# Turning and regrouping y with the first half of tanh, two buffers for the logits' copies, and another order of a chunk's steps

## The chip, the core and the metric

The kernel runs on one core of one Trainium2 chip. Its metric is the device time of one execution in microseconds. The engines of the core are TensorE (PE in the rows, with PEld for its weight loads), VectorE (DVE), ScalarE (ACT), GpSimd (POOL) and SyncE (SP), which issues nearly all transfers here.

## The reference, cut to what matters

```python
# 1. a spectral layer: rfft over 3072 positions, a complex 256x256 mix, soft threshold, irfft
y = np.fft.irfft(shrink(mix(np.fft.rfft(x, axis=1))), axis=1)     # (8, 3072, 256)
x = y.reshape(8 * 3072, 256)                                      # 24576 tokens
# 2. a gated layer without its own activation of the product
h = x @ w_in                                                      # 256 -> 2048
x = (h - np.tanh(h)) @ w_out                                      # 2048 -> 256
# 3. soft mixture of experts, 32 slots
logits = x @ phi
d = softmax(logits, axis=0)          # over the tokens
slot_input = d.T @ x                 # 32 x 256, then 8 small experts
c = softmax(logits, axis=1)          # over the slots
out = c @ slot_out
```

## The kernel before, in words

The program has three stages. `spectral_phase` computes y and stores it in DRAM. `token_phase` goes over the 24,576 tokens in 48 chunks of 512. `expert_phase` runs the experts on the 32 slots and writes the output. Nearly all the text below is about `token_phase`.

The layer after tanh is linear, so the kernel never forms `h - tanh(h)` for all tokens. It needs, for each chunk, g = tanh(h) (eight tiles of 128 x 2 x 512, numbered 0 to 7), the logits from g and from y, and a running sum over the chunks of exp(logits)-weighted g and y. The steps of a chunk c are:

- `P` (L777): products of y and w_in by a Winograd scheme, 28 groups of 6 matmuls; ACT copies the sums out (L788), `A` adds parts on DVE (L795), `G` is tanh on ACT (L799).
- `L` (L915, L923): the logits, from g tiles and from `yr`, a plain copy of y that `loadr` (L806) brings from DRAM.
- `sum`, `sum2`, `max`, `exp`, `turnexp`: the logits are copied to `le`, reduced, exponentiated, and turned to `et`. `comb`, `cexp` and `cend` make the other softmax from the same copy and store it (`ctd`, L1029).
- `T` (L866) turns a g tile by 32x32 blocks on DVE into `gt`; `TD` (L858) does the same with `yr`. There are two `gt` tiles: `gt0` takes tiles 0 to 3, `gt1` takes tiles 4 to 7 and, before the change, y.
- `reg` (L882), once for each half, moves the turned half by 16 transfers from SBUF to SBUF into four `gq` tiles, so that tokens stand on partitions. There are five `gq` buffers; a chunk takes four of them.
- `DY` (L837) multiplies `et` with the y part of `gq`, 32 small matmuls; `D` (L1045) multiplies `et` with the g part, 32 matmuls of 512 columns. They stand next to each other on PE, DY first. `accy` and `acc` add them to the running sums on DVE.

The order of the steps is written by hand in the table `PLAN`: each entry names a step, the chunk it belongs to (0 is the current one, -1 the one before, 1 the next) and which part. Each engine and each queue works its entries off in that order. DY and D of a chunk run near the end of the next chunk's entries. All transfers of this stage go out on SP's queue, one after the other; a transfer that has to wait for an engine holds up those behind it.

Of the kernel before, what the change touches and what calls it, by code (L numbers as in the profile page):

```python
# [9 lines left out]
F32 = mybir.dt.float32  # L10
# [8 lines left out]
S, D = 3072, 256  # L19
# [7 lines left out]


PLAN = (
# [8 lines left out]
    ("reg", -1, 1), ("W", 0, 3), ("splitt", 1, 0), ("comb", -1), ("P", 0, 3, 7),  # L38
# [3 lines left out]
)  # L42
TOKENS_BESIDE = {-4: 1, -2: 1, 0: 1, 1: 2, 2: 3, 3: 4}

# [595 lines left out]
def token_phase(tc, nch, yd, wh, wl, wp, wy, ident, ew):  # L640
# [9 lines left out]
    with ExitStack() as ctx:  # L650
# [73 lines left out]
        gt = {}  # L724
        banks = count()

        def bank():
            k = next(banks) % (4 if ps2 is None else 6)
            return (ps if k < 4 else ps2).tile([128, 512], F32, tag=f"b{k}", name="ph")
# [96 lines left out]
        def dy_mm(c):  # L826


            beside = c < nch - 1
            o = dy[c] = lp[c + 1][:, 256:320] if beside else bank()[:, 0:64]  # L830
            if beside:
                y = [g[:, 2048:2304].rearrange("p (k f) -> p k f", k=4) for g in gq[c]]
            else:
                y = [yq[c][:, a] for a in range(4)]
            for k in range(4):
                for a in (3, 2, 1, 0):
                    nc.tensor.matmul(  # L837
                        o[32 * a:32 * a + 32], ex[c][:, k, :], y[a][:, k], start=k == 0 and not beside, stop=k == 3,
                        skip_group_check=True,
                    )  # L840
# [7 lines left out]

        def gt_tile(c, h):
            if (c, h) not in gt:  # L850
                gt[c, h] = gtp.tile([128, 4, 1024 + 256 * h], F32, tag=f"gt{h}", name="gt", bufs=1)
            return gt[c, h]

        def turn_yr(c):

            t = gt_tile(c, 1)[:, :, 1024:1280].rearrange("p q (k f i) -> p q k f i", k=4, f=2)
            for kk in range(2):
                nc.vector.transpose(  # L858
                    out=t[:, :, :, kk, :], in_=yr[c][:, kk].rearrange("p (q k i) -> p q k i", q=4, k=4)
                )  # L860

        def turn_g(c, p):
            g = gs[c, p]
            t = gt_tile(c, p // 4)[:, :, 0:1024].rearrange("p q (k f i) -> p q k f i", k=4, f=8)
            for u in range(2):
                nc.vector.transpose(  # L866
                    out=t[:, :, :, 2 * (p % 4) + u, :], in_=g[:, u, :].rearrange("p (q k i) -> p q k i", q=4, k=4)
                )

        gq = {}  # L870
# [3 lines left out]
        def regroup(c, h):  # L874

            t = gt.pop((c, h))
            if h == 0:
                gq[c] = [ew.gq_tile([128, 2304]) for _ in range(4)]
            for a in range(4):
                o = gq[c][a][:, 1024 * h:1024 + 1280 * h]  # L880
                for q in range(4):
                    nc.sync.dma_start(out=o[32 * q:32 * q + 32], in_=t[32 * a:32 * a + 32, q])  # L882

# [47 lines left out]
        le = {}  # L931

        def sum_l(c):

            o = lp.pop(c)[:, 0:256]
            if c < nch - 1:
                le[c] = sp.tile([128, 256], F32, tag="le", name="le", bufs=1)
            else:

                last = ew.gp.tile([128, 384], F32, tag="g0", name="last")  # L940
                le[c], ew.rep = last[:, 0:256], last[:, 256:384]
            u = lr[c] = le[c][0:64]
            nc.scalar.activation(u, o[0:64], AF.Copy)
            lo[c] = o
# [88 lines left out]
        def dg_mm(c):  # L1033

            o = dp[c] = ps2.tile([128, 512], F32, tag="d", name="pd")
            if c < nch - 1:
                parts = [(
                    slice(0, 512), [g[:, 0:2048].rearrange("p (h k f) -> p k h f", h=2, k=4) for g in gq.pop(c)],
                )]
            else:  # L1040
                parts = [(slice(256 * h, 256 * h + 256), [gl[h][:, :, a] for a in range(4)]) for h in range(2)]
            for f, g in parts:
                for k in range(4):
                    for a in (3, 2, 1, 0):
                        nc.tensor.matmul(  # L1045
                            o[32 * a:32 * a + 32, f], ex[c][:, k, :], g[a][:, k], start=k == 0, stop=k == 3
                        )
            del ex[c]
# [14 lines left out]
        gtp = ew.gtp  # L1063
# [5 lines left out]
        def do(name, k, *args):  # L1069
            if (name, k, *args) not in done:  # L1070
                done.add((name, k, *args))
                calls[name](k, *args)
# [44 lines left out]
        c = 0  # L1117
        for s in range(8):
            p = FIRST[s]
            if s == 3:  # L1120
                ew.open_mid()
            if s == 5:
                ew.open_late()
                acc, accy, ssum = ew.acc, ew.accy, ew.ssum
                sp = pool("ts", 2)
# [16 lines left out]
            if s == 5:  # L1142
                do("splitt", 1, 0)
                do("splitt", 1, 1)
                split_sw(0)
                do("L", c, 0)
                do("L", c, 2)
            if s == 6:
                sum_w(1, nc.vector, ((ew.txp, "x2"), (ew.txp, "x3")))
                split_sw(1)  # L1150
                do("loadr", c)
                do("reg", c, 0)
                sum_w(2, nc.vector, ((ew.txp, "x0"), (ew.txp, "x1")))
                sum_w(3, nc.gpsimd, ((ew.txp, "x2"), (ew.gqp, "gq4")))
# [3 lines left out]
        c = nch - 1  # L1158
# [364 lines left out]
```

## Time and profile before

| | |
|---|---|
| median of 3 runs | 2242.1 us (2238.6 to 2248.22) |
| the profiled execution | 2236.65 us, span 2234.8 us |
| PE busy | 2169.0 us, 97% of the span |
| DVE busy | 1790.7 us, 80% |
| ACT busy | 1409.0 us, 63% |
| granted clock of TensorE, mean | 0.994 |

The profiled execution is one of several, and its own time is beside its span. Busy shares are averages over the three stages. The busy time of PE counts a matmul from its start to its modelled end, so short pauses between overlapping matmuls do not show in it.

### The profile page before, as it was taken

How to read it: one execution, taken by the hardware profiler on the slowest of the kernel's cores; microseconds unless marked ns; L12 is line 12 of the kernel's file. 1: busy time of each engine (PE TensorE's matmuls, PEld its weight loads, DVE VectorE, ACT ScalarE, POOL GpSimd, SP SyncE). 2: the span in 40 equal slices, each digit the busy share in tenths (PEclk: the TensorE clock that was granted, in tenths of full speed). 3: DMA queues.
4: the chain of work that ended last, by engine and by line, in shares of the span. 5: the costliest groups of instructions: out<-in, count | busy, mean ns of one | idle time of the engine just before them, and what ended most of it. 6: DMA issues, size and time to landing. Idle time of an engine off the chain costs nothing.

```text
span 2234.8 us, 50441 instructions
## 1 busy us (share of the span) xinstructions
PE 2169.0 (97%) x19456; PEld 1771.9 (79%) x19456; DVE 1790.7 (80%) x3651; ACT 1409.0 (63%) x2317; POOL 657.3 (29%) x666
## 2 busy tenths in 40 slices
PE   6999999999999999999999999999999999999998
PEld 3678888888888788888788888888888888888757
DVE  3999888988995888888788888888888888888634
ACT  2456666666555766766666667666666667666624
POOL 0343334444442322222222222222222222222111
PEclk8999999999999999999999999999999999999999
DMA  8778888888657788888788888888888888888999
GB/s 229 229 227 256 269 254 274 249 253 278 198 191 219 187 204 203 198 198 199 193 199 196 202 198 206 196 196 199 198 199 197 194 201 202 194 196 197 265 357 372
DMA packets 259631, 495.75 MB, mean 222 GB/s; under 512 B 36160, under 2 KB 159296, under 8 KB 259008
## 3 DMA queue, kind: packets, MB, share of 16 engines
q1 hardware_dynamic: 259280, 492.49, 81.4%
q8 instruction: 154, 2.52, 0.5%
q14 instruction: 85, 0.70, 0.1%
q10 hardware_dynamic: 112, 0.04, 0.0%
HBM read 164.45 MB, written 106.17 MB: 121 GB/s over the span
## 4 chain that ended last, share of the span: by engine, by line
PE 45%; SPq 8%; DMA 6%; DVE 6%; issue 1%; ACT 1%; POOL 0%; DVEq 0%; POOLq 0%; ACTq 0%
PE ph L777 25%; SPq L882 8%; PE pd L1045 7%; PE pl L915 7%; DMA gq<-gt 4%; DVE gt L866 3%; PE p_out L1344 3%; DVE g L795 2%; DMA ewt<-in_moe_w 2%; PE pl L837 2%; PE pl L923 1%; ACT g L788 1%; DMA gq<-wo 0%; DVE et L991 0%; DMA gq<-in_moe_w 0%
## 5 line engine op out<-in xcount | busy, mean ns | idle before, releaser
L788 ACT ACTIVATE g<-ph 128x512 f32<-128x512 f32 x752 | 447.5, 595 | 411.2 <-PE ph L777 380.6
L795 DVE TENSOR_TENSOR g<-ph,g 128x512 f32<-128x512 f32 x564 | 370.7, 678 | 170.2 <-PE ph L777 119.8
L777 PE MATMUL ph<-th,s 128*128 128x256 f32 x2256 | 486.3, 289 | 1.8 <-ACT g L788 1.8
L866 DVE STREAM_TRANSPOSE gt<-g 128x512 f32<-128x512 f32 x752 | 476.6, 681 | 13.0 <-DMA gq<-gt 6.6
L799 ACT ACTIVATE g<-g 128x1024 f32<-128x1024 f32 x376 | 396.3, 1054 | 32.7 <-DVE g L795 31.2
L777 PEld LDWEIGHTS ph<-th,s 128*128 128x128 f32 x2256 | 377.1, 189 | 35.3 <-issue 19.3
L777 PE MATMUL ph<-tl,s 128*128 128x256 f32 x1128 | 318.3, 282 | 0.0
L777 PE MATMUL ph<-y,wh 128*128 128x256 f32 x1128 | 315.7, 280 | 0.1
L777 PE MATMUL ph<-yh,wh 128*128 128x256 f32 x1128 | 314.9, 279 | 0.5 <-DVE g L795 0.5
L777 PE MATMUL ph<-yh,wl 128*128 128x256 f32 x1128 | 315.4, 280 | 0.0
L690 POOL TENSOR_TENSOR tl<-tr,th 128x512 fp32r<-128x512 f32 x94 | 122.2, 1300 | 378.1 <-ACT th L689 378.1
L372 POOL TENSOR_TENSOR sw<-t,c 64x256 f32<-64x256 f32 x192 | 169.6, 883 | 171.9 <-DVE c L364 141.6
L777 PEld LDWEIGHTS ph<-yh,wh 128*128 128x128 f32 x1128 | 213.0, 189 | 0.8 <-DVE g L795 0.8
L777 PEld LDWEIGHTS ph<-tl,s 128*128 128x128 f32 x1128 | 213.3, 189 | 0.0
L777 PEld LDWEIGHTS ph<-y,wh 128*128 128x128 f32 x1128 | 212.2, 188 | 0.4 <-POOL y L675 0.3
L777 PEld LDWEIGHTS ph<-yh,wl 128*128 128x128 f32 x1128 | 211.9, 188 | 0.0
L684 POOL TENSOR_TENSOR tr<-y 128x256 f32<-128x256 f32 x92 | 68.2, 741 | 424.1 <-DMA y<-yd 424.1
L915 PE MATMUL pl<-g,wp 128*32 128x256 f32 x3072 | 185.9, 382 | 0.0
L1045 PE MATMUL pd<-gq,et 128*32 128x512 f32 x1504 | 175.1, 595 | 0.0
L675 POOL TENSOR_TENSOR y<-y,yh 128x1024 fp32r<-128x1024 f32 x46 | 111.3, 2419 | 214.0 <-PE ph L777 213.9
L407 PEld LDWEIGHTS pi<-i,v 96*128 96x128 f32 x1024 | 127.6, 191 | 25.8 <-issue 20.8
L281 PEld LDWEIGHTS pf<-f,a 128*128 128x128 f32 x768 | 102.8, 196 | 54.4 <-issue 41.1
(224 smaller groups left out, 4467.4 us busy)
## 6 DMA issues: line engine op xcount, KB each, us to landing
gq<-gt SPq DMA_DIRECT2D x752, 160.0 KB, 3.6
gq<-gt SPq DMA_DIRECT2D x752, 128.0 KB, 2.3
xt<-in_x SPq DMA_DIRECT2D x64, 384.0 KB, 5.7
vd<-vs SPq DMA_DIRECT2D x96, 256.0 KB, 3.3
v<-vd SPq DMA_DIRECT2D x64, 384.0 KB, 5.2
yd<-yt SPq DMA_DIRECT2D x48, 512.0 KB, 5.8
y<-yd SPq DMA_DIRECT2D x48, 512.0 KB, 3.7
yr<-yd SPq DMA_DIRECT2D x48, 512.0 KB, 4.9
```

Source lines behind the costliest of these rows:

```text
L372: eng.tensor_tensor(out=v[64 * ri:64 * ri + 64, gg], in0=t[q, e], in1=c[q, e], op=ALU.subtract)
L407: nc.tensor.matmul(p[:, a, :], t[:, 4 * u + a, :], i2[:, 96 * n2:96 * n2 + 128], start=True, stop=True)
L675: eng.tensor_tensor(out=t, in0=yl.pop(c).bitcast(F32), in1=hi.bitcast(F32), op=ALU.subtract)
L690: nc.gpsimd.tensor_tensor(out=lo, in0=t, in1=hi.bitcast(F32), op=ALU.subtract)
L777: nc.tensor.matmul(o[:, 256 * j:256 * j + 256], a[u][:, 128 * j:128 * j + 128], y[v], start=new and j == 0 and k == 0, stop=n in (2, 3, 4) ...
L788: nc.scalar.activation(e[n], o.rearrange("p (j n) -> p j n", j=2), AF.Copy)
L795: nc.vector.tensor_tensor(out=h, in0=o, in1=h, op=ALU.add)
L799: nc.scalar.activation(g, g, AF.Tanh)
L866: nc.vector.transpose(out=t[:, :, :, 2 * (p % 4) + u, :], in_=g[:, u, :].rearrange("p (q k i) -> p q k i", q=4, k=4))
L882: nc.sync.dma_start(out=o[32 * q:32 * q + 32], in_=t[32 * a:32 * a + 32, q])
L915: nc.tensor.matmul(lp[c][q:q + 32, 0:256], wp[:, 2 * p + f, :], half_of(c, gs[c, p + f // 2][:, f % 2], h), start=p == 0 and f < 2, stop=F ...
L1045: nc.tensor.matmul(o[32 * a:32 * a + 32, f], ex[c][:, k, :], g[a][:, k], start=k == 0, stop=k == 3)
```

## The change

The y part of a chunk is turned into `gt0` instead of `gt1`, and goes to the first 256 columns of `gq` with the first half of tanh, instead of the last 256 with the second half. So the 16 transfers of the first half have 1280 columns instead of 1024, and those of the second half 1024 instead of 1280. DY reads the first 256 columns and D the other 2048. `le`, the copy of the logits, has two buffers instead of one. The table `PLAN` is rewritten as a whole; `loadr` now stands near its start and `TD` in its middle, where both stood near its end. In the first chunk, outside the table, `loadr` is issued one step earlier and `TD` runs ahead of the first regrouping.

```diff
-    ("P", 0, 0, 6), ("G", -1, 6), ("L", -1, 2), ("L", -1, 4), ("L", -1, 6), ("cend", -2), ("T", -1, 4), ("T", -1, 7), ("TD", -1), ("loady", 1), ("W", 0, 0),
+    ("S", 0, 2), ("loady", 1), ("T", -1, 4), ("T", -1, 7), ("G", -1, 6), ("W", 0, 0), ("P", 0, 0, 6), ("L", -1, 2), ("L", -1, 4),
...
-                y = [g[:, 2048:2304].rearrange("p (k f) -> p k f", k=4) for g in gq[c]]
+                y = [g[:, 0:256].rearrange("p (k f) -> p k f", k=4) for g in gq[c]]
...
-                gt[c, h] = gtp.tile([128, 4, 1024 + 256 * h], F32, tag=f"gt{h}", name="gt", bufs=1)
+                gt[c, h] = gtp.tile([128, 4, 1280 - 256 * h], F32, tag=f"gt{h}", name="gt", bufs=1)
...
-            t = gt_tile(c, 1)[:, :, 1024:1280].rearrange("p q (k f i) -> p q k f i", k=4, f=2)
+            t = gt_tile(c, 0)[:, :, 0:256].rearrange("p q (k f i) -> p q k f i", k=4, f=2)
...
-            t = gt_tile(c, p // 4)[:, :, 0:1024].rearrange("p q (k f i) -> p q k f i", k=4, f=8)
+            t = gt_tile(c, p // 4)
+            if p < 4:
+                t = t[:, :, 256:1280]
+            t = t.rearrange("p q (k f i) -> p q k f i", k=4, f=8)
...
-                o = gq[c][a][:, 1024 * h:1024 + 1280 * h]
+                o = gq[c][a][:, 1280 * h:1280 + 1024 * h]
...
-                le[c] = sp.tile([128, 256], F32, tag="le", name="le", bufs=1)
+                le[c] = sp.tile([128, 256], F32, tag="le", name="le", bufs=2)
...
-                    slice(0, 512), [g[:, 0:2048].rearrange("p (h k f) -> p k h f", h=2, k=4) for g in gq.pop(c)],
+                    slice(0, 512), [g[:, 256:2304].rearrange("p (h k f) -> p k h f", h=2, k=4) for g in gq.pop(c)],
...
                 do("L", c, 2)
+                do("loadr", c)
...
-                do("loadr", c)
+                do("TD", c)
                 do("reg", c, 0)
```

On SP, in a chunk in the middle of the token stage, the queue before reads as follows: the first half's regrouping (1024 columns), the store of the other softmax, the load of the next y, the second half's regrouping (1280 columns), the load of `yr`.

```order
L882 DMA gq<-gt 32x1024 x16
L1029 DMA ctd<-le 128x128
L664 DMA y<-yd_64 128x1024
L882 DMA gq<-gt 32x1280 x16
L806 DMA yr<-yd_64 128x1024
```

After the change it reads:

```order
L883 DMA gq<-gt 32x1280 x16
L662 DMA y<-yd_64 128x1024
L804 DMA yr<-yd_64 128x1024
L1030 DMA ctd<-le 128x128
L883 DMA gq<-gt 32x1024 x16
```

So the load of `yr` has moved from behind the second half's regrouping to ahead of it, and the store of `ctd` from ahead of y to behind `yr`.

On PE, the end of a chunk before, with what the instructions wait for (DMAHW are the semaphores of transfers): the last logits, DY, D, and the next P.

```order
L915 MATMUL pl<-g,wp 32x256 x8
L837 MATMUL pl<-gq,et 32x64 [waits DMAHW5_49,DMAHW4_49,DMAHW6_49,DMAHW3_49,DVE_49]
L837 MATMUL pl<-gq,et 32x64 [waits DMAHW2_49,DMAHW7_49,DMAHW1_49,DMAHW0_49]
L837 MATMUL pl<-gq,et 32x64 x14
L1045 MATMUL pd<-gq,et 32x512 x16
L777 MATMUL ph<-th,wh 128x256 [waits Activation_49]
```

The same place after the change:

```order
L916 MATMUL pl<-g,wp 32x256 x8
L835 MATMUL pl<-gq,et 32x64 [waits DMAHW5_49,DMAHW4_49,DMAHW6_49,DMAHW3_49,DVE_49]
L835 MATMUL pl<-gq,et 32x64 [waits DMAHW2_49,DMAHW7_49,DMAHW1_49,DMAHW0_49]
L835 MATMUL pl<-gq,et 32x64 x14
L1046 MATMUL pd<-gq,et 32x512 [waits DMAHW6_49,DMAHW7_49,DMAHW1_49,DMAHW0_49]
L1046 MATMUL pd<-gq,et 32x512 [waits DMAHW4_49,DMAHW5_49,DMAHW3_49,DMAHW2_49]
L1046 MATMUL pd<-gq,et 32x512 x14
L775 MATMUL ph<-th,wh 128x256 [waits Activation_49]
```

D has waits for transfers of its own now; before, everything it reads from `gq` had been waited for by DY.

On DVE, the rows around the last turned tile of the second half before (a `gt` row of shape 128x4x4x32 writes the 1280-column tile, L1023 to L1028 are `cend`, L858 is `TD`):

```order
L858 STREAM_TRANSPOSE gt<-yr 128x4x4x32 x2
L795 TENSOR_TENSOR g<-ph,g 128x2x256
L1023 TENSOR_REDUCE cz<-lt 128x4
L1024 TENSOR_SCALAR cz<-cz 128x4
L1025 RECIPROCAL cz<-cz 128x4
L1026 TENSOR_TENSOR lt<-lt,cz 128x128
L1028 STREAM_TRANSPOSE le<-lt 128x128
L866 STREAM_TRANSPOSE gt<-g 128x4x4x32 x4
L795 TENSOR_TENSOR g<-ph,g 128x2x256
L866 STREAM_TRANSPOSE gt<-g 128x4x4x32 x2
```

After the change (the second half is now the tile of shape 128x16x32):

```order
L867 STREAM_TRANSPOSE gt<-g 128x16x32 x2
L793 TENSOR_TENSOR g<-ph,g 128x2x256
L867 STREAM_TRANSPOSE gt<-g 128x16x32 x6
L1024 TENSOR_REDUCE cz<-lt 128x4
L1025 TENSOR_SCALAR cz<-cz 128x4
L1026 RECIPROCAL cz<-cz 128x4
L1027 TENSOR_TENSOR lt<-lt,cz 128x128
L1029 STREAM_TRANSPOSE le<-lt 128x128
L1054 SCALAR_TENSOR_TENSOR acc<-acc,al,pd 128x512
```

The last six transposes of the second half now stand together, ahead of `cend`, and `TD` has left this place.

## Rows read from the trace of the kernel before

**Rows 1.** The page: span, and the busy time of PE and DVE.

```profile
span 2234.8 us, 50441 instructions
PE 2169.0 (97%) x19456; PEld 1771.9 (79%) x19456; DVE 1790.7 (80%) x3651; ACT 1409.0 (63%) x2317; POOL 657.3 (29%) x666
```

**Rows 2.** Busy times in a window, the whole stretch of full chunks; columns first.

```profile
core 0: us, PE busy (x) PEld busy (x) DVE busy (x) ACT busy (x) POOL busy (x), PEclk, DMA share, GB/s
742.00:2077.00 1335.00, 1318.92 (x13696) 1090.77 (x13688) 1094.85 (x2297) 907.13 (x1441) 355.57 (x316) 1.00 0.82 198
```

**Rows 3.** The chain that ended last (start, length, what): some D, one late transfer.

```profile
743.22 3.43 PE pd L1045 x32
...
1094.40 3.65 DMA gq<-gt
1099.06 3.43 PE pd L1045 x31
...
1158.22 3.43 PE pd L1045 x31
...
1168.57 17.15 PE ph L777 x138
...
1187.29 3.43 PE pd L1045 x31
...
1216.51 3.43 PE pd L1045 x31
...
2077.99 3.43 PE pd L1045 x31
```

**Rows 4.** Timeline of PE: DY in two chunks, and the last (brackets: idle before).

```profile
1098.18 0.82 PE L837 MATMUL pl<-gq,et 128*32 128x64 f32 x29 [0.86 <-DMA gq<-gt]
...
1186.56 0.67 PE L837 MATMUL pl<-gq,et 128*32 128x64 f32 x29
1187.02 0.59 PE L1045 MATMUL pd<-gq,et 128*32 128x512 f32 x1
...
2110.78 1.20 PE L837 MATMUL pl<-gq,et 128*32 128x64 f32 x29 [3.42 <-DMA gq<-gt]
```

**Rows 5.** Timeline of SP: one second half, then the queue of another chunk.

```profile
1082.69 12.48 SPq L882 DMA_DIRECT2D gq<-gt  x16
...
1161.69 7.52 SPq L882 DMA_DIRECT2D gq<-gt  x12
...
1169.94 0.38 SPq L664 DMA_DIRECT2D y<-yd  x1
1172.07 11.30 SPq L882 DMA_DIRECT2D gq<-gt  x16
1183.47 0.69 SPq L806 DMA_DIRECT2D yr<-yd  x1
```

**Rows 6.** Timeline of DVE in that chunk, up to the second half's last transpose.

```profile
1164.02 0.69 DVE L795 TENSOR_TENSOR g<-ph,g 128x512 f32<-128x512 f32 x1 [1.73 <-PE ph L777]
1165.38 0.29 DVE L1023 TENSOR_REDUCE cz<-lt 128x4 f32<-128x128 f32 x1 [0.67 <-ACT lt L1018]
...
1166.44 0.31 DVE L1028 STREAM_TRANSPOSE le<-lt 128x128 f32<-128x128 f32 x1
...
1170.75 1.29 DVE L866 STREAM_TRANSPOSE gt<-g 128x512 f32<-128x512 f32 x2
```

**Rows 7.** The page: transfers by line, KB each, median us from issue to landing.

```profile
gq<-gt SPq DMA_DIRECT2D x752, 160.0 KB, 3.6
gq<-gt SPq DMA_DIRECT2D x752, 128.0 KB, 2.3
```

**Rows 8.** Window with the second half's transfers at work (columns as in rows 2).

```profile
1178.00:1184.00 6.00, 6.00 (x50) 5.71 (x49) 5.67 (x13) 5.64 (x11) 1.75 (x1) 1.00 0.98 228
```

**Rows 9.** Groups of ACT in the full chunks: busy, mean ns of one.

```profile
L788 ACT ACTIVATE g<-ph 128x512 f32<-128x512 f32 x720 | 428.5, 595 | 394.6 <-PE ph L777 366.7
L799 ACT ACTIVATE g<-g 128x1024 f32<-128x1024 f32 x361 | 380.6, 1054 | 31.3 <-DVE g L795 29.9
```

More of the change, by code (lines that the diff above doesn't have):

```diff
@@ L29 @@
 PLAN = (
[8 rows of a table removed]
-    ("reg", -1, 1), ("W", 0, 3), ("splitt", 1, 0), ("comb", -1), ("P", 0, 3, 7),
[3 rows of a table removed]
[10 rows of a table added]
 )
```

19 rows, old and new, of the table PLAN are left out of this document.

## The prediction

> **What bounds the kernel now.** I read the page first: PE is busy for 97% of the span and DVE for 80% [rows 1]. The time that a reordering can win is therefore PE's pauses and little else. The windows view shows where to look: the stretch of full chunks in the token stage take 1335 of 2234.8 us, with PE's granted clock at 1.00 throughout and the transfers at a share of 0.82 [rows 2]. The pauses that PE's busy time shows there are 16 us, but matmuls overlap, so a short pause is partly hidden in it.
>
> The chain gives the better measure. From D of the first full chunk to D of the last before the tail it is 2077.99 - 743.22 = 1334.77 us for 45 chunks, 29.66 us each. Where the chain runs through PE alone, a chunk takes less: 1158.22 to 1187.29 is 29.07, and 1187.29 to 1216.51 is 29.22 [rows 3]. So about 0.46 us of a chunk (29.66 - 29.20) is a wait, 45 x 0.46 = 20.7 us in all, and at most 45 x 0.59 = 26.6.
>
> The timeline of PE shows the place. In one chunk DY starts at 1098.18 after an idle time that a transfer into gq ended; the chain has that transfer from 1094.40 for 3.65 us, so it landed at 1098.05, 0.13 before DY. In another chunk DY starts at 1186.56 with no idle time [rows 3, 4]. What lands last is the second half's regrouping: its 16 transfers began at 1082.69 and their issue took 12.48 us; from first issue to last landing that is 15.36 us [rows 5]. And what starts them is DVE: in the chunk of 1158 the y load was issued at 1169.94 to 1170.32, then SP stood for 1.75 us until 1172.07, when the last transposes (1170.75 and 1.29) had ended [rows 5, 6]. Behind the waiting transfer nothing else could go. So the loop is: last P of a chunk, its addition and tanh, cend and six transposes on DVE, 16 transfers, DY.
>
> **The change, part by part.** DY no longer waits for the second half. Its columns come with the first half, which is issued a chunk's length earlier. The wait moves to D, and D's first matmul comes 0.46 us after DY (1187.02 - 1186.56) [rows 4]. That alone is worth the average wait: with the landing where it is, a chunk that waits 0.46 or less waits no more, and the one that waits 0.86 keeps 0.40. PE's own work is the same matmuls, so a chunk without a wait stays at 29.07 to 29.22.
>
> When does the second half land now? I count from D at 1158.22, so the next D's first matmul is due at 29.07 - 0.27 = 28.8 (the chain's row starts 0.27 after it). DY without a wait is 0.46 earlier, at 28.34, or 28.47 in a chunk of 29.20; before, DY came 0.46 later than that on average and the last landing 0.13 ahead of it, so the landing was at 28.8 as well.
>
> Gone is SP's wait for DVE, 1.75 us. cend, from 1165.38 to 1166.75 [rows 6], now stands behind the six transposes and delays only ctd. By DVE's rows the addition at 1164.02 comes about one P later (17.15 us for 23 groups, 0.75 each [rows 3]) and ends near 1165.5; six transposes (3 x 1.29) and cend (1.4) follow, so ctd is ready at about 1170.8, +12.6. SP ends its 12 copies at 1169.21, or 0.9 to 1.8 later by the third point, and y and yr take 0.38 and 0.69 more, so it reaches ctd at +13 to +13.9: DVE is no longer what SP waits for.
>
> Added ahead of the second half is the load of yr. Its issue is 0.69 us; 512 KB (128 x 1024 of 4 bytes) at the 228 GB/s of the busiest window [rows 8] are 2.3 us of the transfer engines. Lower bound of its cost 0.69, upper 2.3.
>
> The 12 first-half copies that wait for D carry 160 KB instead of 128. Twelve of 128 KB took 7.52 us, 0.63 each; sixteen of 160 KB took 11.30 to 12.48, 0.71 to 0.78 each [rows 5]. That is 0.9 to 1.8 us more.
>
> The 16 second-half copies carry 128 KB: 16 x (0.08 to 0.15) = 1.3 to 2.4 us less, and the last lands 2.3 us after its issue instead of 3.6 [rows 7], another 1.3 less when the queue is not full.
>
> With the transfer engines as the limit: -1.75 + 2.3 + 1.7 - 2.3 = -0.05, landing at 28.75. With SP's issue as the limit: -1.75 + 0.69 + 0.9 - 1.3 - 1.3 = -2.8, landing at 26.0. The bad end is slow issue in the first half (+1.8) with none of the relief in the second and 2.3 for yr: +2.35, landing at 31.1. I take 28.4: the share of 0.98 in the busiest window says that it is nearer to the first. That is 0.4 before D, and single chunks scatter by 1 us (15.36 from first issue to landing in one, at most 1186.56 - 1172.07 = 14.49 in another), so I keep 0.1 us a chunk, 4.5 us, as a remaining wait at D.
>
> A rule of the Trainium skill stands against this reading. The row has 228 GB/s at a share of 0.98 with mostly SBUF-to-SBUF copies at work [rows 8]. The page "DMA: Bandwidth & Descriptors", section "Where 436 GB/s comes from", says that such copies are bound by the fabric alone, at 435 GB/s. By it 160 KB would take 0.38 us, the issue would be the limit, the copies would have landed in time before and the change would win nothing; the row says that they are bound at about half that, and I go by the row.
>
> le with two buffers lets sum of a chunk stand ahead of the store of the chunk before. It costs nothing on any engine: copies, reductions and exponentials are as many as before. Its cover is that et must be there for DY. exp now comes after yh and two copies on ACT, then tanh of tile 0, its two transposes, and et. From P 2 6, which yh stands behind, to DY, PE has ten groups, 7.5 us, and the logits of two tiles. The chain on ACT and DVE is three copies (3 x 0.6), two tanh and yh (3 x 1.05), exp with two small companions (about one tanh), two transposes (1.3) and et (two of some 0.3, as L1028) [rows 6, 9]: 7.9 us. It is just hidden by the logits; without that cover each 0.1 us is 4.5 us in all.
>
> TD, T and A in another order: the same number on each engine; DVE is at 82% of this stretch (1094.85 / 1335) [rows 2], so it has 5 us a chunk to wait in. TD stands behind the maximum, two transposes and five additions that follow cend, some 7 us after yr's issue. I put this at nothing; the row of before that is nearest, a chunk of 29.22 without a transfer in its chain against 29.07, says up to 0.15 us a chunk for pauses of another kind, and a gain of as much is the other end.
>
> Ends. In the last chunk DY waits 3.42 us for the second half, which queues behind loads of expert weights [rows 4]. yr goes ahead of it now (+2.3) and its own bytes shrink (-2.3): no gain. The first chunk regroups only after TD. I allow 1 us for both.
>
> Sum: -20.7 + 4.5 + 1 = -15 us against the profiled execution's 2236.65 (span 2234.8 and 1.85 around it): 2221.5. That execution is 5.4 under the median of 2242.1, so the median becomes **2226**.
>
> **Rivals.** Rival 1, most of the wait comes back elsewhere: D waits in half the chunks, or et is late. For it: a margin of 0.4 us at D and hardly one at et. Against: D's part needs several rows at their bad ends. A wait of 0.25 to 0.4 a chunk leaves 3 to 9 us of gain: about 2236.
>
> Rival 2, no change. Either the idle time before DY was not the copies' but another wait's that stays, or D waits as long as DY did, with the landing at 29.3. Against the first: the landing 0.13 before DY [rows 3, 4]. For the second: it is 0.9 from my 28.4. 2242, plus or minus 5. The skill's rule of 435 GB/s would give the first of these; the trace agrees with it in no row shown here.
>
> Rival 3, slower, by SP's queue. From the end of D to the next D there are now 12 copies, y, yr, ctd and 16 copies in one line, and three of these wait for other engines. The same as before results when the landing is at 29.3; the bad end of 31.1 is past it. At 29.7, D comes 1.03 late and a chunk takes 30.1 and the kernel 45 x 0.46 = 20 us more: 2262. The same page of the Trainium skill, section "Anatomy of one DMA — SWDGE (gpsimd) path", says that the engines that move data do not wait on semaphores, only the issuing queue does; the 1.75 us pause of SP agrees.
>
> **Numbers.** Forecast 0.58 (2212 to 2233), rival 1 0.17, rival 2 0.10, rival 3 0.15. The range 2211 to 2250 holds the first three and the beginning of the last. About 0.5%, 11 us, is what a measurement of this kernel can tell from no change. Faster by more: 0.56 of the forecast and 0.06 of rival 1, 0.62. Within: 0.02, 0.11 and 0.08, 0.21. Slower: 0.17.
>
> **What would show it.** Right: DY follows the logits with no idle time in nearly all chunks, D's from one to the next average 29.2 to 29.35, SP goes from ctd to the second half without a pause, starting near +13.5 to +14.5. Wrong: idle time before D of 0.5 us or more on average (rival 3), PE waiting for ACT or DVE inside P (L775) or DY for et (rival 1), or DY still waiting.

## The result, and the profile after

The changed kernel takes 2206.48 us (median of 4 runs, 2203.23 to 2209.54), before 2242.16: a ratio of 0.9838, with a 95% interval of 0.9812 to 0.9864. The forecast was 2226 (2211 to 2250): the sign was right, the gain of 35.7 us is more than twice the 16 forecast, and the time lies under the range. Its profiled execution took 2206.43 us, as much as its median; that of the kernel before lies 5.5 us under its own, so between the two traces below the gain is 30.2 us.

The page, for [rows 1]; then the stretch of full chunks, for [rows 2]:

```profile
span 2204.5 us, 50535 instructions
PE 2140.2 (97%) x19456; PEld 1787.9 (81%) x19456; DVE 1826.2 (83%) x3651; ACT 1398.1 (63%) x2317; POOL 652.4 (30%) x666
```

```profile
744.00:2042.00 1298.00, 1285.43 (x13684) 1103.14 (x13680) 1127.02 (x2295) 896.53 (x1441) 350.78 (x316) 1.00 0.84 204
```

The shares of PE read the same, and the idle time left in the stretch (1298.00 - 1285.43 = 12.6 us, against 16.1) explains 3.5 us of the 37 by which the stretch is shorter (1335 to 1298). The chain shows what a chunk takes now, for [rows 3]:

```profile
744.96 3.67 PE pd L1046 x32
...
1464.92 3.67 PE pd L1046 x32
...
1493.38 3.67 PE pd L1046 x32
...
2043.08 3.85 PE pd L1046 x32
```

From the first to the last it is 1298.12 us for 45 chunks, 28.85 each, against 29.66. A chunk without a wait takes 1493.38 - 1464.92 = 28.46. The least in [rows 3] was 29.07, and the forecast kept that. The timeline of PE, for [rows 4]: one chunk without a wait, and one with it (its D is cut off by the end of the window).

```profile
1290.71 0.63 PE L835 MATMUL pl<-gq,et 128*32 128x64 f32 x32
1291.17 3.84 PE L1046 MATMUL pd<-gq,et 128*32 128x512 f32 x32
...
1319.16 0.63 PE L835 MATMUL pl<-gq,et 128*32 128x64 f32 x32
1320.02 2.31 PE L1046 MATMUL pd<-gq,et 128*32 128x512 f32 x17 [0.23 <-DMA gq<-gt]
```

DY waits for nothing in any of 47 chunks. D does in 26 of 45: here it starts 0.86 after DY instead of 0.46.

Where did the 37 us of the stretch go? On PE, from each matmul's start to the next one's, summed by line and averaged over chunks 2 to 43 (worked out from the start times of both traces):

| PE, us a chunk | before | after | x 45 |
|---|---|---|---|
| P | 20.884 | 20.197 | -30.9 |
| L, with DY's wait behind it | 4.553 | 4.047 | -22.8 |
| DY, with D's wait behind it | 0.658 | 0.810 | +6.8 |
| D | 3.576 | 3.789 | +9.6 |

The last two lines are best read as one: before, three of DY's rows start after D's first and cut its time short, and behind DY's first matmul stands a second wait for transfers (a step between its rows there of 0.18 as a rule, over 0.1 in 41 of 45 chunks, 0.01 to 0.06 in the others). After the change D has waits for transfers too. DY and D together take 4.23 on average before, and 4.23 after where D does not wait; so the 16.4 us that they cost more are nearly all D's wait, 0.35 a chunk.

P, the "same matmuls", gave most. The page can't show it: a matmul of P lasts 0.28 us and the next starts 0.117 later, so a pause of 0.15 is covered by the matmul before. It stands in the start times. Before, P 0 2 1 ends and P 0 1 4 begins, in the timeline of PE and then that of ACT:

```profile
1174.85 0.28 PE L777 MATMUL ph<-yh,wl 128*128 128x256 f32 x1
1175.12 0.38 PE L777 MATMUL ph<-th,wh 128*128 128x256 f32 x1
1175.34 0.28 PE L777 MATMUL ph<-tl,wh 128*128 128x256 f32 x1
```

```profile
1174.46 0.60 ACT L788 ACTIVATE g<-ph 128x512 f32<-128x512 f32 x1 [0.58 <-PE ph L777]
```

P 0 1 4 adds into the bank of P 0 1 7, and ACT reads that bank until 1174.46 + 0.60 = 1175.06. So the first matmul comes 0.27 after the one before instead of 0.117, and the second 0.22 after the first: 0.26 lost. The same happened ahead of P 0 3 6 (0.26). Ahead of P 0 2 7 (0.18) two groups stood between already (P 0 2 5 and P 0 1 3), but ACT had a tanh to do first, so its copy of P 0 2 6, whose last matmul starts at 1177.26, began only at 1178.23. The timeline of ACT before:

```profile
1177.26 1.06 ACT L799 ACTIVATE g<-g 128x1024 f32<-128x1024 f32 x1
1178.23 0.58 ACT L788 ACTIVATE g<-ph 128x512 f32<-128x512 f32 x1
```

P 0 2 7 begins at 1178.86, when that copy has ended (1178.81). The three together are 0.69 a chunk, 31 us. In the new order that tanh (`G 0 3`) stands behind the copy, and two groups instead of one stand between P 0 1 7 and P 0 1 4 and between P 0 3 1 and P 0 3 6. The place ahead of P 0 1 4 has no pause in the timeline of PE after:

```profile
1309.56 0.28 PE L775 MATMUL ph<-yh,wl 128*128 128x256 f32 x1
1309.68 0.28 PE L775 MATMUL ph<-th,wh 128*128 128x256 f32 x1
1309.80 0.28 PE L775 MATMUL ph<-tl,wh 128*128 128x256 f32 x1
```

Below, "excess inside P" is this loss: for each P group the time from the matmul ahead of it to its own last one, less six steps of 0.1167, summed over a chunk. It is 1.69 before and 1.00 after; about 0.82 is the two groups that follow D or the logits in both.

The rest is the wait at D. The timeline of SP in a chunk after, for [rows 5] (the 18 copies in the last row are 16 of this half and 2 of the next), what SP waited for (us in total, times, longest), and the transfers by line, for [rows 7]:

```profile
1303.88 0.69 SPq L662 DMA_DIRECT2D y<-yd  x1
1304.67 1.12 SPq L804 DMA_DIRECT2D yr<-yd  x1
1305.89 0.37 SPq L1030 DMA_DIRECT2D ctd<-le  x1
1306.32 15.25 SPq L883 DMA_DIRECT2D gq<-gt  x18
```

```profile
SPq L883 <- DMA yr<-yd: 65.7, 43, 3.5
```

```profile
gq<-gt SPq DMA_DIRECT2D x752, 160.0 KB, 3.4
gq<-gt SPq DMA_DIRECT2D x752, 128.0 KB, 3.6
...
y<-yd SPq DMA_DIRECT2D x48, 512.0 KB, 5.0
yr<-yd SPq DMA_DIRECT2D x48, 512.0 KB, 6.5
```

The second half starts 14.56 us after the first matmul of the D before (mean of 45), without a wait for DVE. But a copy of it then stands until yr has landed: 65.7 us, 1.5 a chunk. Nothing in that copy depends on yr; in the trace SP's transfers carry eight completion semaphores in turn, and the seventh copy, the eighth transfer behind yr, is the one that takes yr's again (here it starts at 1311.89, yr landed at 1311.88). The half's last landing comes 28.50 after D's first matmul (standard deviation 0.69), and D is due at 28.46.

### The profile page after: what moved, and what is told of

Same layout as the page of the kernel before. It is cut to its first block, busy times and chain, and to the rows that moved or that the text cites. A ratio compares the mean times of both kernels' runs of the same rounds, so it can differ in the third digit from the quotient of the medians.

```text
span 2204.5 us, 50535 instructions
## 1 busy us (share of the span) xinstructions
PE 2140.2 (97%) x19456; PEld 1787.9 (81%) x19456; DVE 1826.2 (83%) x3651; ACT 1398.1 (63%) x2317; POOL 652.4 (30%) x666
## 4 chain that ended last, share of the span: by engine, by line
PE 71%; DMA 12%; SPq 9%; DVE 5%; issue 2%; ACT 1%; POOL 0%; POOLq 0%; DVEq 0%; ACTq 0%
PE ph L775 28%; SPq L883 8%; PE pd L1046 8%; PE pl L916 6%; PE pmix L320 5%; DMA yr<-yd 5%; PE pi L405 5%; PE pf L246 4%; PE pf L279 3%; PE pi L377 3%; PE p_out L1346 3%; PE pa L320 3%; DMA gq<-gt 2%; DMA ewt<-in_moe_w 2%; DVE sw L370 1%
## 5 line engine op out<-in xcount | busy, mean ns | idle before, releaser
L786 ACT ACTIVATE g<-ph 128x512 f32<-128x512 f32 x752 | 440.4, 592 | 342.0 <-PE ph L775 321.4
L867 DVE STREAM_TRANSPOSE gt<-g 128x512 f32<-128x512 f32 x752 | 482.4, 683 | 38.3 <-ACT g L797 30.7
L775 PE MATMUL ph<-th,s 128*128 128x256 f32 x2256 | 477.3, 285 | 5.5 <-ACT g L786 4.5
L797 ACT ACTIVATE g<-g 128x1024 f32<-128x1024 f32 x376 | 390.4, 1052 | 1.8 <-DVE g L793 0.3
L1046 PE MATMUL pd<-gq,et 128*32 128x512 f32 x1504 | 183.0, 599 | 15.7 <-DMA gq<-gt 14.9
L1046 PEld LDWEIGHTS pd<-gq,et 128*32 128x32 f32 x1504 | 89.5, 110 | 71.4 <-issue 18.7
```

Of the source, the lines that this page charges most:

```text
L775: nc.tensor.matmul(o[:, 256 * j:256 * j + 256], a[u][:, 128 * j:128 * j + 128], y[v], start=new and j == 0 and k == 0, stop=n in (2, 3, 4) ...
L786: nc.scalar.activation(e[n], o.rearrange("p (j n) -> p j n", j=2), AF.Copy)
L797: nc.scalar.activation(g, g, AF.Tanh)
L867: nc.vector.transpose(out=t[:, :, :, 2 * (p % 4) + u, :], in_=g[:, u, :].rearrange("p (q k i) -> p q k i", q=4, k=4))
L1046: nc.tensor.matmul(o[32 * a:32 * a + 32, f], ex[c][:, k, :], g[a][:, k], start=k == 0, stop=k == 3)
```

## The experiments

All ratios are to the kernel before, on the same chip. P is named with chunk, column pair and product, as in the table `PLAN`. "Landing" is that of the second half after the first matmul of the D before, mean of 45 chunks.

**The order alone, and y alone.** First the new order with y in its old place (slices, `gt1` and start as before):

```diff
-("W", 0, 2), ("TD", 0), ("A", 0, 1, 3),
+("W", 0, 2), ("A", 0, 1, 3),
...
-("T", 0, 5), ("P", 1, 0, 2),
+("T", 0, 5), ("TD", 0), ("P", 1, 0, 2),
```

> The changed kernel's order of steps, but y is turned into gt1 and regrouped with the second half as before (1024 columns first, 1280 second, DY on the last 256 columns); TD of the current chunk stands behind T 0 5, its only step moved. Theory A (the order of the P groups took away three short pauses a chunk): the pauses ahead of P 0 1 4, P 0 2 7 and P 0 3 6 stay away and a chunk without a wait takes about 28.46 us, but DY waits for the second half again, by 0.5 to 1.5 us a chunk, so the time is 2215 to 2250. Theory B (the shorter chunk comes from the moved y transfers, not from the order): the pauses are back, a chunk without a wait takes 29.07 or more, and the time is 2240 or more.

2274.65 us, ratio 1.0138 (1.0116 to 1.0161): 31 us slower than before. The excess inside P is 0.99, so the order does take the pauses away. But with 1280 columns in the second half and yr ahead of it the landing is at 29.57, and DY waits 1.7 us a chunk, more than the 0.5 to 1.5 expected, so the time is over theory A's 2250 as well. What PE waited for:

```profile
PE pl L835 <- DMA gq<-gt: 59.9, 38, 3.6
```

Then the old order with y in the first half:

```diff
-("L", -1, 6), ("cend", -2), ("T", -1, 4), ("T", -1, 7), ("TD", -1), ("loady", 1),
+("L", -1, 6), ("loadr", 0), ("cend", -2), ("T", -1, 4), ("T", -1, 7), ("loady", 1),
-("W", 0, 2), ("A", 0, 1, 3),
+("W", 0, 2), ("TD", 0), ("A", 0, 1, 3),
...
-("loadr", 0), ("reg", 0, 0), ("G", 0, 7), ("A", 0, 3, 2), ("TD", 0),
+("reg", 0, 0), ("G", 0, 7), ("A", 0, 3, 2),
```

> The order table of before, with y turned and regrouped with the first half; loadr stands behind L -1 6 and TD behind P 0 2 7, since y has to be there for the first half; le keeps one buffer. Theory A: the three pauses stay, a chunk without a wait takes 29.07 to 29.2 us, DY waits no more and D by 0.1 a chunk at most, so 45 x (29.66 - 29.2) = 20 us are won: 2215 to 2228. Theory B: a chunk without a wait takes 28.46 and the time is about that of the changed kernel, 2206.

2250.98 us, ratio 1.0033 (1.0019 to 1.0047): slower, against both theories. DY waits no more and D hardly (0.02 a chunk), as expected, but the excess inside P is 2.37. The new part is 0.56 ahead of P 0 2 3, which waits for an addition that TD now holds up on DVE:

```profile
PE ph L777 <- DVE g L795: 12.8, 45, 0.3
```

(only what exceeds the matmul before counts there, so it reads 0.3 a chunk). So TD was put behind `T 0 0`:

```diff
-("W", 0, 2), ("TD", 0), ("A", 0, 1, 3),
+("W", 0, 2), ("A", 0, 1, 3),
...
-("T", 0, 0), ("G", 0, 2),
+("T", 0, 0), ("TD", 0), ("G", 0, 2),
```

> As the run of y alone, but TD stands behind T 0 0, so that it no longer holds up the addition that P 0 2 3 waits for (0.56 us a chunk there). Theory A: that pause is gone, the three old ones stay, a chunk takes 29.0 to 29.2 us with hardly a wait, and 45 x 0.5 = 22 us are won against before: 2216 to 2226. If instead y in the first half is worth nothing without the new order, the time stays at 2240 or more.

2233.61 us, ratio 0.9963 (0.995 to 0.9977). The three pauses stay (excess 1.86), D waits 0.16 a chunk, the landing is at 28.94. The 0.56 is gone, so TD's place was its cause. y's move in the old order is worth 9 us, less than half of what I expected, and the order alone costs 31; together they win 36. The order makes D due earlier, and y's move takes DY out of the way of the landing.

**The pauses put back.** First one, then all three, by exchanges of neighbours in the changed kernel:

```diff
-("P", 0, 2, 1), ("P", 0, 2, 2), ("P", 0, 1, 4),
+("P", 0, 2, 1), ("P", 0, 1, 4), ("P", 0, 2, 2),
```

> The changed kernel with one pair exchanged: P 0 1 4 ahead of P 0 2 2, so that one group instead of two stands between P 0 1 7 and P 0 1 4, which add into the same bank. Theory A: a pause ahead of P 0 1 4 comes back, a chunk in which D does not wait grows from 28.46 by 0.2 to 0.26 us, D waits less by nearly as much, and the time grows by 2 to 11 us. Theory B: no pause, 28.46, the same time.

2215.78 us, ratio 0.9877 (0.985 to 0.9904), 9 more than the changed kernel. The pause is there (0.25), a chunk without a wait takes 28.72, and D's wait did not shrink (0.34 a chunk, against 0.35): the landing came later too, at 28.76. The intervals of the two ratios touch; the runs themselves do not (2213 and more, against 2210 and less).

```diff
-("P", 0, 1, 3), ("P", 0, 2, 7),
+("P", 0, 2, 7), ("P", 0, 1, 3),
...
-("P", 0, 3, 2), ("P", 0, 3, 5), ("G", 0, 0), ("P", 0, 3, 6),
+("P", 0, 3, 5), ("G", 0, 0), ("P", 0, 3, 6), ("P", 0, 3, 2),
```

(and the exchange above)

> The changed kernel with all three pairs exchanged: P 0 1 4 ahead of P 0 2 2, P 0 2 7 ahead of P 0 1 3, P 0 3 2 behind P 0 3 6, so that one group stands between two that add into the same bank. If the missed part of the gain is these pauses, the excess inside P grows from 1.00 to some 1.7 us a chunk, a chunk without a wait takes 29.1 to 29.25, D waits 0.1 to 0.25 on average since the second half lands 28.5 us after the D before, and the time is 2206 + 45 x (29.3 - 28.85) = 2226, between 2222 and 2236: what was forecast for the change. If not, the time stays under 2215.

2227.35 us, ratio 0.9918 (0.9895 to 0.9941). Excess 1.70, 29.16 a chunk without a wait, D's wait 0.16, landing at 28.60: every number as expected. With a chunk of the length that I assumed, the kernel takes what I forecast for the change. (The pause ahead of P 0 2 7 is made here by one group between instead of two, and is 0.25; the one of before came from the tanh.)

**The pauses taken out of the kernel before.** Three tries, each with more entries moved:

```diff
-("P", 0, 2, 1), ("sum", -1), ("P", 0, 1, 4),
+("P", 0, 2, 1), ("sum", -1), ("P", 0, 2, 2), ("P", 0, 1, 4),
...
-("G", 0, 3), ("rawt", 1), ("sum2", -1), ("P", 0, 2, 2), ("P", 0, 2, 6),
+("rawt", 1), ("sum2", -1), ("P", 0, 2, 6), ("G", 0, 3),
...
-("lowy", 1), ("P", 0, 3, 6), ("turnexp", -1), ("T", 0, 3), ("P", 0, 2, 3),
+("lowy", 1), ("P", 0, 2, 3), ("turnexp", -1), ("T", 0, 3), ("P", 0, 3, 6),
```

> The kernel before with the three pauses alone taken out of the order: P 0 2 2 ahead of P 0 1 4, G 0 3 behind P 0 2 6, P 0 3 6 and P 0 2 3 exchanged. Theory A: the P groups lose some 0.7 us a chunk, but the second half still lands 28.8 us after D as its start hangs on D and DVE, so DY waits 0.5 to 0.7 longer and the time hardly moves: 2232 to 2243. Rival (the pauses are worth their length whatever stands around them): 45 x 0.69 = 31 us less, 2211.

2243.29 us, ratio 1.0003 (0.9988 to 1.0019). The time is as theory A had it, but not for its reason: the excess is 1.78, with 0.51 ahead of P 0 2 3 (an addition on DVE) and 0.29 ahead of P 0 2 6. The second and third try leave P 0 3 6 and P 0 2 3 in their order, and have these instead:

```diff
-("A", 0, 0, 3), ("G", 0, 0),
+("A", 0, 0, 3),
...
-("P", 0, 3, 1), ("A", 0, 2, 7), ("P", 0, 3, 5),
+("P", 0, 3, 1), ("G", 0, 0), ("A", 0, 2, 7), ("P", 0, 3, 2), ("P", 0, 3, 5),
...
-("P", 0, 2, 4), ("A", 0, 2, 3), ("P", 0, 3, 2),
+("P", 0, 2, 4), ("A", 0, 2, 3),
```

> The kernel before with the pauses alone taken out, in another way than the first time (there they came back elsewhere): P 0 2 2 ahead of P 0 1 4, P 0 3 2 ahead of P 0 3 5, G 0 3 behind P 0 2 6 and G 0 0 behind P 0 3 1, so that no tanh stands on ACT between a group and the copy that the next group of its bank waits for. Theory A: the pauses inside P sum to under 0.2 us a chunk instead of 0.70, and DY's wait grows by nearly as much, since the second half lands some 28.8 us after D as before: 2232 to 2243. Rival: the pauses are worth 31 us by themselves, 2213.

2241.15 us, ratio 0.9986 (0.9973 to 0.9998). Excess 2.02: ACT is late with its copies at the chunk's end, 0.76 ahead of P 0 3 7. The third try also moves tanh of tile 2:

```diff
-("G", 0, 2), ("lowy", 1), ("P", 0, 3, 6),
+("lowy", 1), ("P", 0, 3, 6), ("G", 0, 2),
```

> As the second try to take out the pauses alone, with G 0 2 behind P 0 3 6, so that ACT is not behind with the copies of P 0 3 6 and P 0 3 7. If the excess inside P falls under 1.2 us a chunk (1.69 before), the run tells: theory A, the second half lands 28.8 us after D's first matmul as before, DY's wait grows from 0.49 to 0.8 us or more a chunk and the time is 2230 to 2242; rival, the pauses are worth their length, 2211 to 2220. If the excess stays over 1.5, the run tells nothing of them.

2243.59 us, ratio 1.001 (1.0 to 1.0021). The old pauses are gone and 1.03 stands ahead of and in P 1 0 2 (ACT, and POOL's part of the split): excess 2.03. None of the three tells what the pauses are worth in the kernel before; that stays open. In each of them the pauses come back at other places, behind DVE, ACT or POOL.

**What D waits for.** Queue or bytes? The load of yr from POOL, then both loads:

```diff
-nc.sync.dma_start(out=t, in_=yd[c // 6][c % 6])
+(nc.gpsimd if 1 < c < nch - 1 else nc.sync).dma_start(out=t, in_=yd[c // 6][c % 6])
```

> The changed kernel, with the load of yr (chunks 2 to 46) issued by POOL instead of SP; nothing else moves. Theory Q (SP's line is what makes the second half late: its seventh copy stands until yr has landed, 1.5 us a chunk, and yr's issue costs 0.4 to 1.1 more): the second half's issue takes some 10.3 us instead of 12, it lands before D in nearly all chunks, D's wait falls from 0.39 us a chunk on average to 0.1 or less, and the time is 2190 to 2197. Theory T (the transfer engines are full there, shares of 0.9 to 1.06, and whichever queue asks, the bytes take as long): the landing stays, D waits 0.3 to 0.45 a chunk, 2203 to 2210.

2224.28 us, ratio 0.993 (0.9901 to 0.9959): slower than the changed kernel, so theory Q falls; theory T's time (2203 to 2210) was missed too. SP no longer stands for yr, but longer for y, whose median landing went from 5.0 to 7.6 us:

```profile
SPq L883 <- DMA y<-yd: 92.2, 45, 3.7
```

```profile
y<-yd SPq DMA_DIRECT2D x48, 512.0 KB, 7.6
yr<-yd POOLq DMA_DIRECT2D x45, 512.0 KB, 5.7
```

The landing is at 28.88 and D waits 0.59 a chunk. The Trainium skill says the same ("DMA: Bandwidth & Descriptors", section "Issuing engines are not separate DMA queues"): transfers of all issuers share the same engines, and a second issuer saves only the issuing time. The trace agrees: with yr off SP's line the second half lands no earlier (28.88, against 28.50).

The same edit in `load_y` as well:

> The changed kernel with both loads, y and yr (chunks 2 to 46), issued by POOL. Theory Q: as with yr alone or 1 to 4 us better, since SP issues 32 copies and ctd alone and no copy stands behind a 512 KB load: 2186 to 2196. Theory T: 2203 to 2210. If POOL is late in its line (it splits weights and y's low parts), y or yr come late and P or the logits wait: over 2215.

2270.87 us, ratio 1.0112 (1.0088 to 1.0136): the third case. The 16 copies take longer to issue (13.4 us, against 12.0), though hardly one stands behind y or yr any more; they stand behind earlier copies and ctd (83.7 and 30.6 us in all). And yr comes so late (8.4 us from POOL's issue) that TD blocks DVE and P 0 1 3 loses 1.2 us a chunk:

```profile
PE ph L775 <- DVE g L793: 44.0, 32, 2.9
```

So fewer bytes: the load of yr cut, then replaced.

```diff
+            n = 64 if 1 < c < nch - 1 else 512
+            if n == 64:
+                nc.gpsimd.memset(t[:, :, 64:512], 0.0)
-            nc.sync.dma_start(out=t, in_=yd[c // 6][c % 6])
+            nc.sync.dma_start(out=t[:, :, 0:n], in_=yd[c // 6][c % 6][:, :, 0:n])
```

> The changed kernel with the load of yr cut to 64 of 512 columns (POOL sets the others to zero), in chunks 2 to 46, at the same place of SP's line: the logits' and the softmax's y part are left out for the rest. It keeps the place in the line and takes away 448 KB. Theory T: as without the load, D waits under 0.05 us a chunk, 2188 to 2195. Theory Q (the place in SP's line): the landing moves by under 0.7 us, 2200 to 2206.

2189.63 us, ratio 0.9766 (0.9751 to 0.978): theory T. (The kernel leaves out most of y's part of the logits, so it only measures.) D waits 0.04 a chunk, no copy stands for yr, the 16 copies issue in 10.9 us, and the landing is at 27.73, which is 0.77 earlier. That is less than the 2 us that 448 KB take at the 228 GB/s of [rows 8]: the copies then go one behind the other at SP's pace, 0.68 us each on average.

```diff
-            nc.sync.dma_start(out=t, in_=yd[c // 6][c % 6])
+            hi, lo = ys[c]
+            nc.gpsimd.tensor_tensor(out=t, in0=hi.bitcast(F32), in1=lo.bitcast(F32), op=ALU.add)
```

> The changed kernel without the load of yr: POOL makes it as the sum of yh and of the low part of y, which lie in SBUF in the chunk that needs it. So 512 KB a chunk go from SP's line and from the transfer engines. Theory T (the second half is late since the transfer engines have too many bytes ahead of it): at 228 GB/s the 512 KB are 2.3 us, the second half lands 2 us earlier, D waits under 0.05 us a chunk instead of 0.35, and the time is 2188 to 2194. Rival (its landing hangs on D's end, DVE and SP's pace of 0.64 us a copy, not on bytes): the landing moves by 0.5 us at most and the time is 2200 to 2206; if POOL is late with yr, the logits or TD wait: over 2210.

2230.75 us, ratio 0.9947 (0.9929 to 0.9964), over both theories' ranges. The landing is at 27.73 too and D waits 0.01. But P 0 0 3 now waits 0.9 us a chunk for an addition on DVE. The timelines of DVE and POOL show why:

```profile
1346.67 0.18 DVE L1027 RECIPROCAL cz<-cz 128x4 f32<-128x4 f32 x1
1346.88 2.52 DVE L1028 TENSOR_TENSOR lt<-lt,cz 128x128 f32<-128x128 f32 x1
1349.44 0.31 DVE L1030 STREAM_TRANSPOSE le<-lt 128x128 f32<-128x128 f32 x1
```

```profile
1346.86 2.39 POOL L805 TENSOR_TENSOR yr<-yh,y 128x1024 f32<-128x1024 f32 x1 [2.69 <-issue]
```

cend's multiplication takes 0.29 us elsewhere and here as long as POOL's addition beside it. So cend was moved ahead of the last two transposes:

```diff
-("T", -1, 7), ("G", -1, 6),
+("T", -1, 7), ("cend", -2), ("G", -1, 6),
...
-("T", -1, 6), ("cend", -2), ("acc", -2),
+("T", -1, 6), ("acc", -2),
```

> The changed kernel with yr made on POOL, and cend moved from behind T -1 6 to behind T -1 7, so that its multiplication on DVE (2.52 us beside POOL's addition, 0.29 before) is done when POOL makes yr. If that was the cause of the pause of 0.9 us ahead of P 0 0 3, the pause goes, a chunk takes 28.46 to 28.55 us, D waits under 0.05, and the time is 2187 to 2194. If POOL holds up DVE's transposes and additions too, P still waits for DVE by 0.3 us or more a chunk: 2203 to 2225.

2190.41 us, ratio 0.9769 (0.9755 to 0.9784), and a chunk of 28.47: 16 us less than the changed kernel and 52 less than the one before. In its DVE and POOL timelines the two no longer meet, and the page has PE at 98%:

```profile
1325.20 0.29 DVE L1028 TENSOR_TENSOR lt<-lt,cz 128x128 f32<-128x128 f32 x1
```

```profile
1326.36 2.41 POOL L805 TENSOR_TENSOR yr<-yh,y 128x1024 f32<-128x1024 f32 x1 [2.69 <-issue]
```

```profile
PE 2135.3 (98%) x19456; PEld 1784.8 (82%) x19456; DVE 1826.6 (84%) x3651; ACT 1398.1 (64%) x2317; POOL 768.4 (35%) x714
```

**The ends.** In the changed kernel PE idles for 4.54 us at the start of chunk 1, where ACT's `split_sw` 2 waits for DVE ahead of the copies of P. That step was put back:

```diff
-("S", 0, 2), ("loady", 1),
+("loady", 1),
...
-("G", 0, 1), ("P", 0, 0, 3),
+("G", 0, 1), ("S", 0, 2), ("P", 0, 0, 3),
```

> The changed kernel with split_sw 2, which runs in chunk 1 alone, put back behind G 0 1, where it stood before. If its wait for DVE's sums at the start of chunk 1 is what holds the copies of P back there (PE idle for 4.53 us), the first DY comes 3 to 6 us earlier and the time is 2200 to 2204; the rival (the sums are late anyway and PE waits for them a few groups later): the same time within 1.5 us.

2212.61 us, ratio 0.986 (0.9845 to 0.9874): no gain, and over both cases; the interval overlaps that of the changed kernel. The timeline of PE has the wait in pieces and later:

```profile
724.21 0.39 PE L775 MATMUL ph<-th,s 128*128 128x256 f32 x1 [2.58 <-ACT g L786]
...
737.52 0.58 PE L775 MATMUL ph<-th,s 128*128 128x256 f32 x1 [5.19 <-ACT g L786]
```

The last chunk's load of yr, and its first expert loads, behind the regrouping:

```diff
-if k < nch - 1 or name not in ("T", "TD", "reg"):
+if k < nch - 1 or name not in ("T", "TD", "reg", "loadr"):
-("W", 0, 0), ("P", 0, 0, 6),
+("P", 0, 0, 6),
...
-("W", 0, 1),
+("W", 0, 1), ("W", 0, 0),
```

> The changed kernel with the last chunk's load of yr and the first loads of expert weights and ctd behind the second half's regrouping of the chunk before, in chunk 47 alone. If that line on SP is what holds the last D beside a full chunk up (3.6 us), it waits under 0.5 us and the time is 1 to 4 us less, 2202 to 2205; the rival (the experts then wait for those loads at the end): no gain, 2205 to 2210.

2205.74 us, ratio 0.9836 (0.9819 to 0.9852): the last D beside a chunk waits no more (3.59 us before the edit), the time is the same. Beside yr on chip, with the same move of the first loads:

> As the run with yr on chip and cend first, and in the last chunk the first loads of expert weights and ctd stand behind the second half's regrouping. The last D beside a full chunk waits under 0.3 us; the time is the same within 4 us, since moving those loads gained nothing in the changed kernel.

2192.35 us, ratio 0.9776 (0.9762 to 0.9791): again nothing.

**le with one buffer:**

```diff
-("loadr", 0), ("sum", -1), ("P", 0, 0, 7), ("P", 0, 1, 1), ("T", -1, 6), ("cend", -2), ("acc", -2),
+("loadr", 0), ("P", 0, 0, 7), ("P", 0, 1, 1), ("T", -1, 6), ("cend", -2), ("sum", -1), ("acc", -2),
-tag="le", name="le", bufs=2)
+tag="le", name="le", bufs=1)
```

> The changed kernel with one buffer for le; so that it can be, sum of the chunk before stands behind cend instead of ahead of P 0 0 7, and ACT's copy of the logits waits for the store of ctd. If the second buffer is what lets et be ready for DY (7.9 us of work for 7.5 us of cover, by the forecast), DY or the logits wait and the time is 2215 or more; if it is hidden, 2204 to 2210. Forecast: the chain to et starts later by the store of ctd, some 6 us after SP reaches it, so ACT holds up the copies behind sum: over 2215.

2518.44 us, ratio 1.12 (1.1158 to 1.1243). The run changes two things, since one buffer forces sum behind cend. ACT's copy of the logits stands for the store of ctd, 6.7 us a chunk, and P's copies behind it:

```profile
ACT le L944 <- DMA ctd<-le: 310.4, 46, 11.0
```

The granted clock fell with these pauses, to 0.92 in 1300 to 1360, a mean between the two levels of 1.2 and 2.4 GHz; what that adds to the time is not separated here. In the changed kernel it is 1.00 in the full chunks.

## Why the prediction was wrong in size, point by point

**DY's wait goes: right.** None of 47 chunks waits there; the table has -22.8 us ahead of DY, I had -20.7. That agrees partly by luck: I took the chunk of 29.22 as one without a wait, but DY's second wait stood in it (the step of 0.18). With that wait DY lost 0.65 a chunk, 29 us and not 20.7. D, from its first matmul to the next P, is 0.16 longer now (3.79, before 3.63), which takes 7 us back; that its new waits do this is likely, but not tested.

**The second half's landing: right.** I put it at 28.4 after D's row in the chain, which starts 0.27 after D's first matmul, so at 28.67; it is 28.50. SP goes from ctd to the copies without a pause, at +14.56 by the same count (forecast +13.5 to +14.5 from the row). The parts of that sum were off, though: yr costs more than its bytes (a copy stands 1.5 us for its landing), and the copies of 128 KB land 3.6 us after issue instead of 2.3. That the sum came out all the same is luck.

**"PE's own work is the same matmuls, so a chunk without a wait stays at 29.07 to 29.22": this step failed.** It falls to 28.46, since P lost 0.69 us of pauses; I took P's 0.75 a group for its own length, where 0.70 is. I put this term at nothing, and it is -31 us, of which D's longer wait takes some 11 back. With pauses of that size put back the kernel takes 2227, so this step makes up nearly the whole error of the sum (2227.35 against 2226); that it fits to 1.4 us is closer than the other terms allow. "Right" was to be 29.2 to 29.35 from one D to the next; it is 28.85. I had the row for it: 23 groups in 17.15 us, 0.75 each [rows 3], beside six steps of 0.117.

**"0.4 before D", 4.5 us of wait left: failed with it.** D is due at 28.46 instead of 29.07, so the margin of 0.4 became -0.04, and with a scatter of 0.69 D waits 0.35 on average. That is 16 us instead of 4.5.

**le and the path to et: right, the reason too.** I had et "just hidden by the logits". It is ready 0.55 us before DY starts (0.54 at the least), where it was 3.3 before the change. The timeline of DVE after; this et is ready at 1318.62 and its DY starts at 1319.16:

```profile
1317.99 0.63 DVE L992 STREAM_TRANSPOSE et<-le 64x128 f32<-64x128 f32 x2
```

And the second buffer is no side matter: without it, and with sum behind cend, ACT waits for ctd and the kernel takes 312 us more.

**TD and the additions at nothing: right for this order, by luck of its place.** TD in the middle of the old order costs 0.56 us a chunk (e2).

**The ends at +1: 6 in these two traces.** The first full DY came 1.7 us later and the stretch from the last full DY to the end is 4.3 longer (162.0 against 157.7). Traces of other versions scatter between 157.3 and 162.1 there, so whether the change did it stays open.

**Rivals.** The wait did come back at D, as rival 1 had it, in half of the chunks (0.35 a chunk, within its 0.25 to 0.4). It did not set the time, since P gave 31 us that no case of mine held. Rivals 2 and 3 did not come: the time fell by 35.7 us, and SP's longer line did not make the second half later. A wait that is cut and a chunk that gets shorter meet at the same place: in the landing of the second half.

## What to carry to other kernels

Before calling the matmuls "the same work", divide a chain's row by its groups and compare with the pitch of matmuls that wait for nothing: where matmuls overlap, a wait of 0.15 us shows as no idle time, and what it costs shows only in the start times. Where another engine must copy a bank between two groups that add into it, look at two things: how many groups of other banks stand between, and what that engine has to do ahead of the copy. Here one group between cost 0.25 to 0.26 us each time; two cost nothing when the copy came at once, and 0.18 when a tanh stood ahead of it. And when a transfer bounds a loop, moving it to another queue may only change which copy stands, as it did here; taking its bytes away changed the time.

## What the runs showed of the hardware

A multiplication of two SBUF operands on DVE, 128 x 128, took 0.29 us alone and 2.52 beside a 2.39 us addition on POOL, while the transposes and the additions that read one operand from PSUM kept their times. The Trainium skill has this rule ("SBUF — State Buffer", section "Who interferes with whom"): a DVE instruction with two SBUF inputs contends with a GpSimd instruction that reads SBUF. The trace agrees, and comb's subtraction in the changed kernel (1.15 us on average, 0.29 at its shortest and before the change) beside POOL's part of y does too.

A pause on PE cost more than the wait: after it the next step took 0.22 us instead of 0.117, at each of the three places. The copies of the second half were paced by SP at 0.64 us each, 0.59 for the issue itself, whenever nothing else held them.
